# Pooled-query attention with a routed expert: score and value matmuls on four 64x64 tiles, chunk by chunk in turn

## The chip, the cores and the metric

One core of a Trainium2 chip runs the whole program, everything in float32. The metric is the time of one execution on the device in microseconds (us), lower is better. Five engines work side by side, each through its own instructions in order: TensorE (PE; its weight loads are listed apart as PEld), VectorE (DVE), ScalarE (ACT), GpSimd (POOL) and SyncE (SP), which here issues DMAs. TensorE writes into PSUM, from which ScalarE and VectorE read.

## The reference

Attention on queries that are averaged two by two, 8 batches of 8 heads, 1152 keys, head dimension 64. Then, for each batch, the 128 of 576 tokens with the highest gate score go through a two-layer expert and are added back.

```python
def _attn_ref(q, k, v):
    B, H, S, D = q.shape                     # 8, 8, 1152, 64
    scale = 1.0 / np.sqrt(D)
    q_pool = q.reshape(B, H, S // 2, 2, D).mean(axis=3)
    scores = scale * np.matmul(q_pool, k.transpose(0, 1, 3, 2))
    scores = scores - np.max(scores, axis=-1, keepdims=True)
    attn = np.exp(scores)
    attn = attn / (np.sum(attn, axis=-1, keepdims=True) + 1e-09)
    return np.matmul(attn, v).astype(np.float32)
...
def _moe_ref(x, w_gate, w1, w2, capacity):   # x: 8, 576, 512; w1: 512 x 1024; capacity 128
    scores = np.einsum('bsd,d->bs', x, w_gate)
    out = x.copy()
    for b in range(B):
        top_idx = np.argpartition(-scores[b], capacity)[:capacity]
        xe = x[b, top_idx]
        h = np.maximum(xe @ w1, 0.0)
        ye = h @ w2
        g = 1.0 / (1.0 + np.exp(-scores[b, top_idx]))
        out[b, top_idx] = x[b, top_idx] + g[:, None] * ye
```

## The kernel before

Two heads of a batch form a pair; there are 32 pairs. A pair lies in the 128 partitions as 2 heads of 64: kT and qT hold the transposed keys and pooled queries, head j in the rows 64j to 64j+63. The 576 queries of a pair are worked through in two halves of 288 (`s` is 0 or 1), so there are 64 halves, numbered h in `run`. The 1152 keys are 9 chunks of 128.

`scores` takes a half through all 9 chunks. For each chunk and head, a matmul with 64 rows of kT as weights (64 rows by 128 columns of the array) gives the transposed scores of 128 keys by 288 queries; the two heads use the two halves of the array's rows and write into the two banks of one PSUM tile. ScalarE turns the tile into exponentials (L763) in `p`. There is no maximum subtracted; at the end a count of sums outside bounds decides whether a second, general version (`_any_scores`) has to run, which it doesn't with these inputs. `weighted` takes a half through the 9 chunks again: with the values as weights (128 rows by 64 columns) and `p` as the moving operand, the two heads use the two halves of the array's columns and accumulate in one PSUM bank, which ScalarE copies out (L779). A float32 matmul is two instructions on TensorE, each with its weight load, so each of the two runs has 36 matmuls in the profile.

PSUM has one pool, `psum`, with 4 tiles of two banks each, that is all 8 banks; `banks()` (L893) hands them out in turn, to scores, values, the sums' matmul, the transposes and the expert alike. A tile is used again when its last reader is done.

The order is written out by hand in `run`; each engine works through its part of it in order. One turn h of the loop issues:

- `scores(h)`; `gated(h-3)`, a small reduction on VectorE of gate products, and for the second half of a pair another (L880); after a batch's last pair it starts that batch's routing;
- `folded(h)`: GpSimd adds p's first and second group of three chunks (L788, three sums), VectorE folds the third group and then those sums over the keys (L793, two instructions), and adds up (L802). The first of these folds reads the chunks 6 to 8, the second the three sums of GpSimd;
- `multiplied(h-2)`: GpSimd multiplies attention outputs by the gate weights (L825);
- where h is even, `prepare_pair` for the next pair: keys transposed on VectorE (L727), queries summed on GpSimd (L733) and transposed on VectorE (L739);
- `weighted(h-1)` and `drained(h-1)`: VectorE transposes the copied values into `avb` (L815);
- where h-1 was a pair's second half, `normalized`: a matmul merges the sums (L836), ScalarE copies them out (L846, two instructions), VectorE takes reciprocals (L853), GpSimd scales (L855, the tile `x`), and SyncE stores `x` in the next turn;
- `units`: each batch in routing does its next piece, the newest batch first.

The routing of a batch is a generator, `routed`, in pieces: the gate scores are brought into a row (L916, L920 and DMAs through memory), VectorE compares them to find ranks (L970, L979, L989), over three turns, and in the third makes five `pick` matrices from the ranks (L1012); a turn later TensorE multiplies these by token numbers (L1022) and ScalarE reads out indices (L1030, L1032); GpSimd gathers the tokens with an indirect DMA (L1034); later come four transposes (L1048) and their copy (L1051), the first expert layer (L1059, 64 matmuls, ReLU L1067), and the second (L1072, 16 matmuls, read by L1092), a scaled sum and a scatter. The last batch's routing, and what is left of the one before, run after the loop, the pieces of both interleaved by hand; there the gate scores become a row through matmuls (L943, L950, L671).

Of the kernel before, what the change touches and what calls it, by code (L numbers as in the profile page):

```python
# [10 lines left out]
P = 128  # L11
BLK = 32

G = 3
F32 = mybir.dt.float32
I32 = mybir.dt.int32
AF = mybir.ActivationFunctionType
ALU = mybir.AluOpType
# [516 lines left out]
class _Plain:  # L535
# [10 lines left out]
    def __init__(self, ctx, tc, q, k, v, moe_w_gate, moe_w1, moe_w2, capacity, out):  # L546
        self.tc, self.nc = tc, tc.nc
        self.q, self.k, self.v, self.out = q, k, v, out
        self.w_gate_in, self.w1_in, self.w2_in = moe_w_gate, moe_w1, moe_w2
        B, H, S, D = q.shape  # L550
        self.B, self.H, self.S, self.D = B, H, S, D
        self.Sp = S // 2
        self.Dm = H * D
        self.F = moe_w1.shape[1]
        self.NC = S // P
        self.NPAIR = H // 2
        self.HALF = self.Sp // 2
        self.QB = self.Sp // BLK
        self.HB = self.HALF // BLK
        self.KB = S // BLK  # L560
        self.NF = self.Sp // P
        self.TAIL = self.Sp - self.NF * P
        self.NT = self.NF + 1
        self.ND = self.Dm // P
        self.NFC = self.F // P
        self.NG = self.NC // G
        self.scale = 0.5 / math.sqrt(D)
        self.slots = [(s, min(P, capacity - s)) for s in range(0, capacity, P)]

        assert tuple(out.shape) == (B, self.Sp, self.Dm)  # L570
        assert 2 * D == P and D == 2 * BLK and H == 2 * self.NPAIR
        assert S == self.NC * P and self.NC == self.NG * G and self.NG == 3
        assert self.HALF == self.HB * BLK and self.HALF <= 512
        assert 0 < self.TAIL < P and self.Dm == self.ND * P and self.Dm <= 512
        assert self.F == self.NFC * P and self.NFC % 4 == 0
        assert all(w > 1 for _, w in self.slots) and capacity < self.Sp

        def pool(name, bufs, **kw):
            return ctx.enter_context(tc.tile_pool(name=name, bufs=bufs, **kw))

        self.const = pool("const", 1)
        self.load = pool("load", 2)
        self.work = pool("work", 2)
        self.small = pool("small", 4)
        self.ffn = pool("ffn", 2)
        self.dram = pool("dram", 2, space=bass.MemoryType.DRAM)
        psum = bass.MemoryType.PSUM
        self.psum = pool("psum", 4, space=psum)
        self.constants()

    def quarters(self):
# [152 lines left out]
            for a, z in parts:  # L744
                of(a, z)

    def scores(self, half):

        nc, pair, n = self.nc, half["pair"], self.HALF
        qs = slice(half["s"] * n, (half["s"] + 1) * n)  # L750
        p = half["p"] = self.work.tile([P, self.NG, G, 2, n], F32, name="p")
        for c in range(self.NC):
            sc = self.banks()
            for j in range(2):
                rows = slice(j * self.D, (j + 1) * self.D)
                nc.tensor.matmul(  # L756
                    sc[:, j, 0:n],
                    lhsT=pair["kT"][rows, c * P : (c + 1) * P],
                    rhs=pair["qT"][rows, qs],
                    start=True,  # L760
                    stop=True,
                )
            nc.scalar.activation(p[:, c // G, c % G, :, :], sc[:, :, 0:n], AF.Exp, scale=self.scale)  # L763

    def weighted(self, half):

        nc, n = self.nc, self.HALF
        av = self.banks()[:, 0, :]
        for c in range(self.NC):
            for j in range(2):  # L770
                nc.tensor.matmul(  # L771
                    av[j * self.D : (j + 1) * self.D, 0:n],
                    lhsT=half["pair"]["v"][:, j, c, :],
                    rhs=half["p"][:, c // G, c % G, j, :],
                    start=(c == 0),
                    stop=(c == self.NC - 1),
                )
        half["av"] = self.small.tile([P, n], F32, name="av", bufs=2)
        nc.scalar.copy(half["av"][:, :], av[:, 0:n])  # L779

    def folded(self, half):

# [25 lines left out]

    def drained(self, half):

        pair, hb = half["pair"], self.HB
        if half["s"] == 0:
            pair["avb"] = self.work.tile([P, self.QB, BLK], F32, name="avb")
        ns = slice(half["s"] * hb, (half["s"] + 1) * hb)
        self.nc.vector.transpose(  # L815
            pair["avb"][:, ns, :].rearrange("p n d -> p (n d)"), half["av"][:, :]
        )

    def multiplied(self, half):
# [329 lines left out]
    def run(self):  # L1149
        nc = self.nc  # L1150
        pairs = [(b, hp) for b in range(self.B) for hp in range(self.NPAIR)]
        n_halves = 2 * len(pairs)
        halves = []
        self.routing = []
        first = ((4, self.KB // 2, self.KB), (self.HB, self.QB))
        upcoming = self.load_pair(*pairs[0], parts=first, other=nc.scalar)
# [2 lines left out]
        loaded = self.load_pair(*pairs[1]) if len(pairs) > 1 else None  # L1159
        weights = self.weight_loads()  # L1160
        for h in range(n_halves + 1):
            if h < n_halves:
                n, s = divmod(h, 2)
                if s == 0:
                    pair = upcoming
                    if pair["hp"] == 0:
                        xs = self.dram.tile([self.Sp, self.Dm], F32, name="xs")
                        part = self.ffn.tile([P, self.NPAIR, self.QB], F32, name="part")
                    pair.update(xs=xs, part=part)
                else:  # L1170
                    loaded = self.load_pair(*pairs[n + 2]) if n + 2 < len(pairs) else None
                    if n > 0:
                        self.stored(halves[h - 2]["pair"])
                if h > 1:
                    next(weights, None)
                half = {"pair": pair, "s": s}
                halves.append(half)
                self.scores(half)
                if h > 2:
                    self.gated(halves[h - 3])  # L1180
                self.folded(half)
                if h > 1:
                    self.multiplied(halves[h - 2])
                if s == 0 and loaded:
                    upcoming = loaded
                    self.prepare_pair(upcoming)
            else:
                if h > 2:
                    self.gated(halves[h - 3])
                self.multiplied(halves[h - 2])  # L1190
                self.units()
            if h > 0:
                done = halves[h - 1]
                self.weighted(done)
                self.drained(done)
            if h == n_halves:
                self.multiplied(done)
                self.gated(halves[h - 2])
            if h > 0 and done["s"] == 1:
                self.normalized(done["pair"])  # L1200
            if h < n_halves:
                self.units()
        for _ in weights:
# [92 lines left out]
```

## Time and profile before

| | |
|---|---|
| median of 3 runs | 747.36 us (747.1 to 750.39) |
| the profiled execution | 747.73 us |
| its span in the profile | 746.0 us |
| granted TensorE clock, mean | 0.999 |
| TensorE matmuls, busy | 728.5 us, 5465 instructions |
| VectorE, busy | 518.8 us, 760 instructions |
| GpSimd, busy | 429.4 us, 396 instructions |
| ScalarE, busy | 388.0 us, 769 instructions |
| score matmuls L756 | 2304, busy 299.7 us |
| value matmuls L771 | 2304, busy 293.5 us |
| exponentials L763, 128x576 | 576, mean 685 ns |
| copies of values L779, 128x288 | 64, mean 400 ns |
| folds L793 | 128, means 1969 and 1951 ns |
| sums on GpSimd L788, 128x576 | 192, mean 1413 ns |

The span runs from the first to the last instruction of the program in the profile; the time on the device holds 1.7 us more. Matmuls are pipelined, and the length of one reaches from its start to the end of its passage through the array, so a run of n matmuls is read by the starts. A row of the timeline merges neighbours of the same line: start, length from the first start to the last end, engine, line, operation, tiles, shapes and count; in brackets the idle time of the engine before, and who ended it. In a row of windows the columns are the stretch, its length, and busy time and count of an engine, followed by clock, DMA share and GB/s.

### The profile page before, as it was taken

To read this page: it belongs to the slowest core of one execution; us is meant where nothing else is said; L and a number is where in the kernel's file an instruction comes from. 1 tells how busy PE (TensorE), PEld (TensorE's weight loads), DVE (VectorE), ACT (ScalarE), POOL (GpSimd) and SP (SyncE) were. 2 spreads that over 40 slices of the span, in tenths; PEclk is the share of its full clock that TensorE was granted. 3 is DMA by queue.
4 is the path that set the end of the run, shared out by engine and by line. 5 is a ranking of instruction groups with operands and counts; after the bars stand their busy time and mean duration, and the time that the engine had idled before them with its cause. 6 is when DMAs were issued, how large, how long until landed. Compare 5 with 4: busy or idle time off the path is not lost. (4 is left out here: it accounts for less than half of the span.)

```text
span 746.0 us, 14111 instructions
## 1 busy us (share of the span) xinstructions
PE 728.5 (98%) x5465; PEld 490.6 (66%) x5465; DVE 518.8 (70%) x760; ACT 388.0 (52%) x769; POOL 429.4 (58%) x396
## 2 busy tenths in 40 slices
PE   6899999999999999999999999999999999999986
PEld 4566666677566675676756767566676677666764
DVE  1766668977389753997549975498855978469640
ACT  3566666654465644666336664465535664366320
POOL 5666666664566736657556466465655655376520
PEclk9999999999999999999999999999999999999999
DMA  8999998995298646978279682995929966271130
GB/s 129 152 193 186 178 188 121 155 140 126 49 163 138 98 108 83 159 108 127 80 113 151 86 126 81 144 146 85 109 84 152 145 99 110 68 115 17 31 95 33
DMA packets 459310, 87.09 MB, mean 117 GB/s; under 512 B 455520, under 2 KB 455520, under 8 KB 458976
## 3 DMA queue, kind: packets, MB, share of 16 engines
q1 hardware_dynamic: 455008, 81.53, 70.4%
q0 software_dynamic: 1280, 4.20, 2.1%
q8 instruction: 45, 0.74, 0.5%
q10 hardware_dynamic: 2944, 0.36, 0.3%
q14 instruction: 33, 0.27, 0.1%
HBM read 74.50 MB, written 20.99 MB: 128 GB/s over the span
## 5 line engine op out<-in xcount | busy, mean ns | idle before, releaser
L763 ACT ACTIVATE p<-ps 128x576 f32<-128x576 f32 x576 | 319.9, 685 | 19.6 <-PE ps L756 12.8
L788 POOL TENSOR_TENSOR acc<-p 128x576 f32<-128x576 f32 x192 | 265.8, 1413 | 90.2 <-ACT p L763 89.7
L756 PE MATMUL ps<-qT,kT 64*128 64x288 f32 x2304 | 299.7, 410 | 7.7 <-DVE qT L739 7.7
L771 PE MATMUL ps<-p,v_sb 128*64 128x288 f32 x2304 | 293.5, 409 | 0.0
L756 PEld LDWEIGHTS ps<-qT,kT 64*128 64x128 f32 x2304 | 223.7, 188 | 73.1 <-issue 18.5
L771 PEld LDWEIGHTS ps<-p,v_sb 128*64 128x64 f32 x2304 | 159.8, 137 | 125.6 <-ACT p L763 24.2
L793 DVE TRANSPOSE_TENSOR_REDUCE fold<-p 128x54 f32<-128x1728 f32 x64 | 126.0, 1969 | 122.8 <-ACT p L763 122.8
L793 DVE TRANSPOSE_TENSOR_REDUCE fold<-acc 128x54 f32<-128x1728 f32 x64 | 124.9, 1951 | 55.6 <-POOL acc L788 55.6
L779 ACT COPY av<-ps 128x288 f32<-128x288 f32 x64 | 25.6, 400 | 214.9 <-PE ps L771 214.9
L855 POOL TENSOR_TENSOR x<-avb,rec 128x576 f32<-128x576 f32 x32 | 37.0, 1158 | 146.0 <-DVE rec L853 133.9
L1059 PEld LDWEIGHTS ps<-xeT,w 128*128 128x128 f32 x512 | 58.0, 192 | 3.7 <-issue 2.6
L1059 PE MATMUL ps<-xeT,w 128*128 128x128 f32 x512 | 59.7, 277 | 0.7 <-ACT xeT L1051 0.7
L1072 PE MATMUL ps<-w,hT 128*128 128x512 f32 x128 | 57.0, 597 | 0.0
L825 POOL TENSOR_TENSOR prod<-avb,w_gate 128x288 f32<-128x288 f32 x64 | 50.9, 795 | 3.9 <-DVE avb L815 3.9
L733 POOL TENSOR_TENSOR qp<-qb 128x576 f32<-128x576 f32 (+1 forms) x33 | 45.0, 1362 | 9.8 <-DMA qb<-in_q_dram 9.7
L727 DVE STREAM_TRANSPOSE kT<-kb 128x1152 f32<-128x1152 f32 (+3 forms) x34 | 44.0, 1296 | 4.6 <-DMA kb<-in_k_dram 4.3
L1012 DVE TENSOR_SCALAR pick<-slot_f,rank 128x128 f32<-128x128 f32 (+1 forms) x40 | 41.9, 1110 | 0.4
L1072 PEld LDWEIGHTS ps<-w,hT 128*128 128x128 f32 x128 | 23.6, 190 | 26.3 <-issue 26.1
L1067 ACT ACTIVATE hT<-ps 128x512 f32<-128x512 f32 x16 | 9.6, 597 | 50.6 <-PE ps L1059 50.6
L880 DVE TENSOR_TENSOR part<-red,rec 128x18 f32<-128x18 f32 x32 | 33.6, 1050 | 1.1
L739 DVE STREAM_TRANSPOSE qT<-qp 128x576 f32<-128x576 f32 (+1 forms) x33 | 23.8, 721 | 10.9 <-POOL qp L733 10.9
L815 DVE STREAM_TRANSPOSE avb<-av 128x288 f32<-128x288 f32 x64 | 29.0, 453 | 1.1 <-ACT av L779 1.1
(71 smaller groups left out, 276.4 us busy)
## 6 DMA issues: line engine op xcount, KB each, us to landing
v_sb<-in_v_dram SPq DMA_DIRECT2D x64, 288.0 KB, 5.0
kb<-in_k_dram SPq DMA_DIRECT2D x124, 144.0 KB, 4.3
qb<-in_q_dram SPq DMA_DIRECT2D x124, 144.0 KB, 4.6
xs<-x SPq DMA_DIRECT2D x128, 72.0 KB, 3.1
out_dram<-xs SPq DMA_DIRECT2D x8, 1152.0 KB, 5.6
w<-in_moe_w_dram SPq DMA_DIRECT2D x8, 512.0 KB, 5.0
sc_row<-row SPq DMA_DIRECT2D x7, 288.0 KB, 3.3
qb<-in_q_dram ACTq DMA_DIRECT2D x4, 72.0 KB, 2.7
```

The source lines that it names most:

```text
L727: nc.vector.transpose(pair["kT"][:, a * BLK : z * BLK], pair["k"][:, a:z, :].rearrange("p n d -> p (n d)"),)
L733: nc.gpsimd.tensor_tensor(out=qp[:, a:z, :], in0=pair["q"][:, a:z, 0, :], in1=pair["q"][:, a:z, 1, :], op=ALU.add,)
L756: nc.tensor.matmul(sc[:, j, 0:n], lhsT=pair["kT"][rows, c * P : (c + 1) * P], rhs=pair["qT"][rows, qs], start=True, stop=True,)
L763: nc.scalar.activation(p[:, c // G, c % G, :, :], sc[:, :, 0:n], AF.Exp, scale=self.scale)
L771: nc.tensor.matmul(av[j * self.D : (j + 1) * self.D, 0:n], lhsT=half["pair"]["v"][:, j, c, :], rhs=half["p"][:, c // G, c % G, j, :], star ...
L788: nc.gpsimd.tensor_tensor(out=acc[:, u, :], in0=units[:, 0, u, :], in1=units[:, 1, u, :], op=ALU.add)
L793: nc.vector.tensor_reduce(fold[:, a, :], of.rearrange("p u (m d) -> p (u m) d", d=BLK), AX.X, ALU.add, apply_transpose=True,)
L825: self.nc.gpsimd.tensor_tensor(out=pair["prod"][:, ns, :], in0=pair["avb"][:, ns, :], in1=self.w_gate[:, hp : hp + 1, :].broadcast_to([P, ...
L855: nc.gpsimd.tensor_tensor(out=x[:, :, :], in0=pair["avb"][:, :, :], in1=rec[:, :].unsqueeze(2).broadcast_to([P, self.QB, BLK]), op=ALU.mult,)
L1012: nc.vector.tensor_scalar(out=pick[0:rows, t, 0:w], in0=self.slot_f[0:rows, s0 : s0 + w], scalar1=rank[0:rows, t : t + 1], scalar2=None, o ...
L1059: nc.tensor.matmul(pv[:, f, 0:w], lhsT=self.w1[:, c, (f0 + f) * P : (f0 + f + 1) * P], rhs=xeT[:, c, 0:w], start=(c == 0), stop=(c == self ...
L1072: nc.tensor.matmul(ps[0:w, 0 : self.Dm], lhsT=hT[:, f, 0:w], rhs=self.w2[:, f, :], start=(f == 0), stop=(f == self.NFC - 1),)
```

## The change

`scores` and `weighted` become one function, `attended(half, done)`. For each chunk it issues the scores of the present half, the exponential, and then the values of the half before, for the same chunk. Each matmul is split in two: the scores by keys (64 of the chunk's 128, that is 64 columns of weights), the values by keys too (64 rows of weights), so that every matmul has a 64x64 tile of weights and the same 288 columns to move. A chunk's scores are then four matmuls on the four quarters of the array, and so are its values. The two halves of the keys of the values accumulate in two PSUM banks; both are copied out in one instruction, 576 columns instead of 288, and GpSimd adds them (a new instruction in `drained`), ahead of the transpose. PSUM is divided into two pools: 2 tiles of two banks for scores and everything else, and 2 for values. In `run` the values of h-1 now come ahead of `gated`, `folded`, `multiplied` and `prepare_pair`. In the turn after the last half, `units` comes ahead of the values.

```diff
@@ -585,7 +585,8 @@
-        self.psum = pool("psum", 4, space=psum)
+        self.psum = pool("psum", 2, space=psum)
+        self.ps_av = pool("ps_av", 2, space=psum)
@@ -744,39 +745,45 @@
-    def scores(self, half):
...
-    def weighted(self, half):
...
+    def attended(self, half, done):
+        nc, n = self.nc, self.HALF
+        quarters = [(slice(e * self.D, (e + 1) * self.D), e, j) for e in range(2) for j in range(2)]
+        if half:
+            pair = half["pair"]
+            qs = slice(half["s"] * n, (half["s"] + 1) * n)
+            p = half["p"] = self.work.tile([P, self.NG, G, 2, n], F32, name="p")
+        if done:
+            av = self.ps_av.tile([P, 2, 512], F32, name="av")
         for c in range(self.NC):
+            if half:
+                sc = self.banks()
+                for keys, e, j in quarters:
+                    rows = slice(j * self.D, (j + 1) * self.D)
+                    nc.tensor.matmul(
+                        sc[keys, j, 0:n],
+                        lhsT=pair["kT"][rows, c * P + keys.start : c * P + keys.stop],
+                        rhs=pair["qT"][rows, qs],
+                        start=True,
+                        stop=True,
+                    )
+                nc.scalar.activation(
+                    p[:, c // G, c % G, :, :], sc[:, :, 0:n], AF.Exp, scale=self.scale
+                )
+            if done:
+                for keys, e, j in quarters:
+                    nc.tensor.matmul(
+                        av[j * self.D : (j + 1) * self.D, e, 0:n],
+                        lhsT=done["pair"]["v"][keys, j, c, :],
+                        rhs=done["p"][keys, c // G, c % G, j, :],
+                        start=(c == 0),
+                        stop=(c == self.NC - 1),
+                    )
+        if done:
+            done["av"] = self.small.tile([P, 2, n], F32, name="av", bufs=2)
+            nc.scalar.copy(done["av"][:, :, :], av[:, :, 0:n])
@@ -808,12 +815,16 @@
     def drained(self, half):
-        pair, hb = half["pair"], self.HB
+        pair, hb, av = half["pair"], self.HB, half["av"]
+        total = self.small.tile([P, self.HALF], F32, name="av_sum", bufs=2)
+        self.nc.gpsimd.tensor_tensor(
+            out=total[:, :], in0=av[:, 0, :], in1=av[:, 1, :], op=ALU.add
+        )
...
-            pair["avb"][:, ns, :].rearrange("p n d -> p (n d)"), half["av"][:, :]
+            pair["avb"][:, ns, :].rearrange("p n d -> p (n d)"), total[:, :]
@@ -1175,29 +1187,27 @@
-                self.scores(half)
-                if h > 2:
-                    self.gated(halves[h - 3])
+            if h == n_halves:
+                self.units()
+            done = halves[h - 1] if h else None
+
+            self.attended(half, done)
+            if h > 2:
+                self.gated(halves[h - 3])
+            if half:
                 self.folded(half)
-                if h > 1:
-                    self.multiplied(halves[h - 2])
-                if s == 0 and loaded:
-                    upcoming = loaded
-                    self.prepare_pair(upcoming)
...
+            if h > 1:
                 self.multiplied(halves[h - 2])
-                self.units()
-            if h > 0:
-                done = halves[h - 1]
-                self.weighted(done)
+            if half and half["s"] == 0 and loaded:
+                upcoming = loaded
+                self.prepare_pair(upcoming)
+            if done:
                 self.drained(done)
-            if h == n_halves:
-                self.multiplied(done)
-                self.gated(halves[h - 2])
-            if h > 0 and done["s"] == 1:
-                self.normalized(done["pair"])
+                if h == n_halves:
+                    self.multiplied(done)
+                    self.gated(halves[h - 2])
+                if done["s"] == 1:
+                    self.normalized(done["pair"])
             if h < n_halves:
                 self.units()
```

## The prediction

> **What bounds the kernel now.** I read the page first, for the shares of the engines; then the timeline of one stretch in the middle of the run; then the list of waits; then the timelines of VectorE and GpSimd over the same stretch, because a reordering of TensorE's work changes when theirs can begin.
>
> ```profile
> span 746.0 us, 14111 instructions
> ...
> PE 728.5 (98%) x5465; PEld 490.6 (66%) x5465; DVE 518.8 (70%) x760; ACT 388.0 (52%) x769; POOL 429.4 (58%) x396
> ```
>
> TensorE has work for 98% of the span, so whatever changes its busy stretch changes the time. The timeline shows what this stretch is made of:
>
> ```profile
> 301.19 4.64 PE L756 MATMUL ps<-qT,kT 64*128 64x288 f32 x36
> ...
> 305.76 4.59 PE L771 MATMUL ps<-p,v_sb 128*64 128x288 f32 x36
> ...
> 310.27 0.41 PE L836 MATMUL ps<-sum,merge 128*128 128x36 f32 x2
> 310.39 0.40 ACT L779 COPY av<-ps 128x288 f32<-128x288 f32 x1 [3.35 <-PE ps L771]
> 310.62 4.64 PE L756 MATMUL ps<-qT,kT 64*128 64x288 f32 x36
> 310.72 0.56 ACT L846 ACTIVATE sums<-ps,tiny 64x18 f32<-64x18 f32 x2
> ...
> 315.18 4.59 PE L771 MATMUL ps<-p,v_sb 128*64 128x288 f32 x36
> ...
> 319.70 4.64 PE L756 MATMUL ps<-qT,kT 64*128 64x288 f32 x36
> ```
>
> Columns are start, length, engine, line, operation, count. A half is 36 score matmuls and 36 value matmuls; each half starts 9.08 us after the one before where nothing stands between (310.62 to 319.70) and 9.43 us where the sums' matmul L836 does (301.19 to 310.62). The pace inside a run comes from a piece cut out of one:
>
> ```profile
> 321.74 2.59 PE L756 MATMUL ps<-qT,kT 64*128 64x288 f32 x20
> ...
> 329.02 1.23 PE L1022 MATMUL ps<-meta,pick 128*128 128x3 f32 x9
> ```
>
> One such matmul has a length of 0.40, so 20 of them take (2.59 - 0.40)/9 = 0.243 us per pair: two run at once, in the two halves of the array. The expert matmuls L1072, one at a time with 512 columns, follow each other by 0.43 us, and 288/512 of that is 0.242. So the pair is paced by the array, not by loading or issuing. 36 pairs at 0.243 are 8.74 us; the other 0.34 us of a direct half are the changes between the two forms of matmul. From 28.3 to 694.3 us, 62 halves, TensorE has no other pause. VectorE looks idle by its 70%, but not in the stretch in which a batch's tokens are ranked:
>
> ```profile
> 297.99 1.98 DVE L793 TRANSPOSE_TENSOR_REDUCE fold<-p 128x54 f32<-128x1728 f32 x1 [9.62 <-ACT p L763]
> ...
> 323.31 6.01 DVE L1012 TENSOR_SCALAR pick<-slot_f,rank 128x128 f32<-128x128 f32 x5
> 329.24 0.43 DVE L878 TENSOR_REDUCE red<-prod 128x9 f32<-128x288 f32 x1
> ```
>
> ```profile
> 297.90:329.30 31.40, 30.70 (x55) 1.00 1.06 143
> ```
>
> In the second view (VectorE's own windows) it is busy 30.70 of 31.40 us, beginning with the fold of the half whose scores started at 292.11. The picks end at 329.3, and the last of the matmuls that read them (L1022, from 329.02) begins at about 330.0. There are some 0.6 us to spare.
>
> **The change, part by part.** *Matmuls.* Each of 72 matmuls of a half becomes two on a 64x64 tile with the same 288 columns. If four run at once, a quad takes the pair's 0.243 us, and a half keeps its 36 steps, 8.74 us. I take this, since both neighbours are in the trace: two tiles that share rows (the values) and two that share columns (the scores) both go at full pace. What goes is the change of form: 0.34 us per direct half. Where L836 or an expert stage stands between, some 0.15 of it stays as the way back into the attention form (9.43 - 9.08 = 0.35 is paid for L836 as now), so 0.19 is saved. Of 62 halves, 31 have L836 behind them and 6 an expert stage: 25 x 0.34 + 37 x 0.19 = **-15.5 us**.
>
> [...]
>
> *Twice the instructions.* Eight loads and matmuls have to issue in 0.243 us, 30 ns each. The trace shows only that 61 ns each is kept up (4 per pair), and over the 128 instructions of an expert stage 56 ns. Bounds: nothing, and a doubling of every step (8.74 x 62 = +542 us). I take nothing, because the pace above is exactly the array's, so the issuing was not at its limit; the other end is a rival.
>
> *Two PSUM buffers instead of four* for scores and everything else. L836 then writes into the buffer of chunk 7, and what comes two tiles later needs its reader L846 to be done. Now L846 ends 311.28, which is 1.34 us after the start of the last value pair (305.76 + 4.59 - 0.41 = 309.94). The copy before it grows from 288 columns to 576 (0.40 to about 0.69, the length of an exponential of 576), and an exponential is still ahead of it (0.1): 1.73 us. Where only L836 stands between, its successor needs the buffer a chunk later (0.97 us) and waits under 0.1. With the four transposes L1048 behind, the next scores would start at 1.3: 0.17 for the last exponential's buffer and 0.4 for L846. With L916 and L1072 behind, L1072 would start at 0.97: 0.17 and 0.72. Per batch 0.07 + 0.57 + 0.89 = 1.5 us, 7 batches: **+10.6 us**, bounds 0 (should the exponentials' early part take it up) and 14.
>
> *Chunks in turn.* The last exponential of a half now comes at the half's end. In the stretch above, the first fold started 5.88 us after its scores' first matmul (297.99 - 292.11); with 9 chunks of 0.97 us (scores and values of a chunk, two quads each) it starts at 8.74 + 0.44 = 9.18. VectorE works through the same list in order, without a pause to catch up in, so its end, the picks, comes 3.3 us later. TensorE arrives at L1022 some 0.9 us earlier (two direct halves, one with L836, one up to L1022, less 0.1 for the buffers). Minus the 0.6 to spare: L1022 waits 3.6 us, and in TensorE's queue the next half's scores and all else stand behind it. 7 such stretches lie inside the loop: **+25 us**. Bounds: a pick takes 1.2 us here while GpSimd runs sums beside it, but in the tail, with GpSimd quiet, five took 1.06 together:
>
> ```profile
> 718.12 1.06 DVE L1012 TENSOR_SCALAR pick<-slot_f,rank 128x128 f32<-128x128 f32 x5
> ```
>
> Five quick picks would take 4.9 us off and end the wait: 0. Above: the added sums on GpSimd hold up each pick and fold once more (0.8 us twice), and after a pause of 6 us at the start the first six pairs took 0.48 instead of 0.24, 1.4 us if it happens after this one: 7 x 6.6 = 46. I take the middle one because GpSimd will be just as full there: three sums of 1.4, a product of 0.8, a query sum of 1.4, now another 0.8.
>
> *The added sum* (L825's form, 128x288, 0.8 us x 64) lies on GpSimd, busy 58%, behind the value copy; in the loop only x and the products come later for it, which have a half to spare. In the tail it is on the path. There the chain is: last copy, transpose, product, ranks, picks:
>
> ```profile
> 705.25 0.48 DVE L815 STREAM_TRANSPOSE avb<-av 128x288 f32<-128x288 f32 x1 [1.13 <-ACT av L779]
> ```
>
> It starts 0.29 (longer copy) + 0.8 + 0.1 later, and with two buffers the count's matmul L1127 waits for the read of the old expert result, 0.5: **+1.7 us**. The first 28 us end with the second pair's queries, which come from memory: 0. DMAs and their queues issue the same transfers in the same order.
>
> Sum, against the profiled execution's own 747.7 us (746.0 span and 1.7 around it; the median of the three is 747.36): 747.7 - 15.5 + 10.6 + 25 + 1.7 = **769.5 us**.
>
> **Rivals.** *The late folds cost nothing* (other side). If picks miss GpSimd's sums, L1022 waits under 0.46 us a batch; that is the point at which -15.5 + 10.6 + 1.7 = -3.2 is used up. Then 744.5, and 734 if the buffers wait for nothing: 740. For it: a pick's price hangs on where GpSimd is just then. Against it: GpSimd's list there grows.
>
> *Four tiles don't run at once, or can't be fed.* Two at a time: 747.7 + 542 = 1290; a quad of 0.30 instead of 0.243: +127, 875. For it: no row shows more than two tiles, or instructions faster than 56 ns for long. Against it: the exact pace of the array in both present forms.
>
> *The alternation itself costs.* If the present 0.34 us belongs to the change of operands and not of tile form, a half pays it nine times instead of once: 8 x 0.34 x 62 = +169, 917. For it: no row has scores and values in one form. Against it: L836, followed by L1022 with other operands in the same form, keeps the 0.11 us of its neighbours.
>
> **How the numbers follow.** Full pace with late folds 0.57, between 752 and 790 for itself. Late folds free 0.22. Not four at once 0.08, alternation 0.06. The remaining 0.07 is a draw of gain and waits near the old time. What a measurement can tell from no change is 0.5%, 743.6 to 751.1. Faster: 0.21. Within: 0.10. Slower: 0.69. The range reaches from the middle of the rival on the other side, 738, to 795; below it lies some 0.06, above it 0.14.
>
> **What would show it.** Right: runs of 72 matmuls in which four start within some 10 ns, quads every 0.243 us, no pause between scores and values; VectorE's first fold 9.2 us behind its half's start; TensorE waiting some 3.6 us for picks at L1022, seven times; short waits for L846 and L920's buffers. Wrong: quads above 0.25 us, a pause at every chunk, L1022 without a wait, or waits of the scores for the exponentials inside a half, which I count at nothing because a chunk (0.97 us) exceeds an exponential (0.69) and its buffer is wanted again only 1.94 us later.

## The result, and the profile after

The changed kernel is slower: a median of 782.44 us over 4 runs (781.3 to 783.15) against 747.23 us (746.41 to 750.39), a ratio of 1.0462 [1.0428, 1.0495]. The profiled execution took 783.15 us. This is the top of its page; the rows of the second part are tenths of 40 slices, here the clock that TensorE was granted:

```profile
span 781.4 us, 23357 instructions
...
PE 742.7 (95%) x10073; PEld 465.9 (60%) x10073; DVE 494.8 (63%) x760; ACT 448.0 (57%) x769; POOL 478.6 (61%) x460
...
PEclk8999999899998999989999899998999989999998
```

The clock has become part of the story: a dip about every 95 us, which is once per batch. The granted clock averages 0.965 instead of 0.999. TensorE's share fell to 95%, so there are pauses as well. First the attention itself, in the timeline of TensorE (start, length, engine, line, operation, tiles, shapes, count; in brackets the idle time before and who ended it):

```profile
310.42 0.67 PE L765 MATMUL ps<-qT,kT 64*64 64x288 f32 x8
310.90 0.66 PE L777 MATMUL av<-p,v_sb 64*64 64x288 f32 x8
311.39 0.66 PE L765 MATMUL ps<-qT,kT 64*64 64x288 f32 x8
```

Each row holds eight instructions, two for each of four tiles, and the rows follow each other by 0.485 us, so a quad (four instructions, one for each tile) starts every 0.2425 us. The single starts show the four of a quad within some 20 ns, and 72 quads (two halves' worth, scores and values of nine chunks) in 17.29 us from first to last start, where 71 x 0.2425 is 17.22. So four tiles do run at once, eight loads and matmuls do issue in the 0.2425 us of a quad, and going from scores to values costs nothing. A direct half takes 8.78 us (the starts of its first scores are 301.64 and 310.42) where it took 9.08, and one with L847 behind it 9.19 (310.42 to 319.61) where it took 9.43. The same timeline where a batch's tokens are picked:

```profile
336.65 0.67 PE L777 MATMUL av<-p,v_sb 64*64 64x288 f32 x8
337.24 0.41 PE L847 MATMUL ps<-sum,merge 128*128 128x36 f32 x2
338.05 0.35 PE L1033 MATMUL ps<-meta,pick 128*128 128x3 f32 x2 [0.39 <-DVE pick L1023]
338.71 0.38 PE L1033 MATMUL ps<-meta,pick 128*128 128x3 f32 x2 [0.31 <-DVE pick L1023]
340.06 0.39 PE L1033 MATMUL ps<-meta,pick 128*128 128x3 f32 x2 [0.97 <-DVE pick L1023]
340.81 1.11 PE L1033 MATMUL ps<-meta,pick 128*128 128x3 f32 x4 [0.36 <-DVE pick L1023]
341.84 1.24 PE L765 MATMUL ps<-qT,kT 64*64 64x288 f32 x8
342.86 1.18 PE L777 MATMUL av<-p,v_sb 64*64 64x288 f32 x8
...
347.41 0.66 PE L765 MATMUL ps<-qT,kT 64*64 64x288 f32 x8
```

Two things are to be seen. L1033 (the old L1022) waits for one pick after another, and the next half's scores stand behind it: from L847 to the scores pass 4.6 us. And the scores and values behind them then follow each other by 1.02 and 0.96 us where 0.485 was the pace: for 44 matmuls, 5.3 us, TensorE runs at half its clock, until about 347.1. The windows of all engines say the same (stretch, its length, then busy time and count of PE, PEld, DVE, ACT and POOL, clock, DMA share, GB/s), and the third row, of TensorE alone, bounds the stretch:

```profile
329.00:338.00 9.00, 8.65 (x142) 5.20 (x134) 8.51 (x17) 6.74 (x13) 8.92 (x10) 1.00 0.86 135
338.00:347.00 9.00, 7.32 (x54) 4.67 (x58) 8.93 (x11) 2.05 (x8) 2.66 (x3) 0.63 0.57 99
```

```profile
340.31:347.14 6.83, 6.47 (x50) 0.50 0.43 81
```

The clock already falls while the last picks are read. The trace has six such stretches of 6.83 us inside the loop, behind the first six batches' picks, and one of 3.41 behind the seventh's.

VectorE and GpSimd are both full ahead of the picks. Their rows, from the fold with which the batch's last ranking begins:

```profile
310.86 1.98 DVE L800 TRANSPOSE_TENSOR_REDUCE fold<-p 128x54 f32<-128x1728 f32 x1 [10.44 <-ACT p L772]
...
335.41 1.12 DVE L1000 SCALAR_TENSOR_TENSOR tie<-sc_row,gate_sc,before 64x64 f32<-64x64 f32 x1
336.78 4.16 DVE L1023 TENSOR_SCALAR pick<-slot_f,rank 128x128 f32<-128x128 f32 x5
340.87 0.43 DVE L889 TENSOR_REDUCE red<-prod 128x9 f32<-128x288 f32 x1
```

```profile
333.68 4.14 POOL L795 TENSOR_TENSOR acc<-p 128x576 f32<-128x576 f32 x3
337.78 0.79 POOL L836 TENSOR_TENSOR prod<-avb,w_gate 128x288 f32<-128x288 f32 x1
338.54 1.38 POOL L734 TENSOR_TENSOR qp<-qb 128x576 f32<-128x576 f32 x1
339.89 0.78 POOL L820 TENSOR_TENSOR av_sum<-av 128x288 f32<-128x288 f32 x1
```

The fold starts 9.22 us after its half's first score (301.64). The picks end at 340.9, just after GpSimd's last row here. They are shorter than before, 4.16 us for the five instead of 6.01 (L1012 at 323.31 in the view before), and the single rows of the two engines say why. Four of the picks end at 337.90, 338.65, 340.01 and 340.75, each 0.08 to 0.09 us behind the end of one of GpSimd's last four instructions here, and the fifth, with GpSimd done, takes 0.27 us. Before, all five picks ended so behind an instruction of GpSimd: the three sums, the product and the query sum. So a later start lets the picks miss two of the sums, and the added sum gives them one instruction more to wait behind.

Where the 35.4 us between the spans (781.4 - 746.0) lie, each from the starts in the two traces, the first as what is left (the shorter halves above are its direct evidence):

| place | us | how read |
|---|---|---|
| steady attention, changes of form gone | -14.5 | remainder |
| waits for the two PSUM buffers | +10.7 | after L927, 0.977 to the next start (before 0.111 or 0.194), 7 times; after L1059, 0.725 (0.203), 6 times; from L847 to L927 or L1059, 0.22 (0.11), 13 times |
| waits for the picks | +20.6 | from the last L847 to the next scores 4.44 to 4.63, in the seventh batch 2.93 (before 1.32); of this, the ten starts of L1033 span 3.51 and 2.09 (1.10) |
| half clock after the picks | +17.2 | the two-half block after each takes 19.77 to 19.93 instead of 17.30; the last one 1.69 more |
| tail, from the last L847 | +1.86 | 43.16 (41.30) |
| start | -0.5 | the third half begins at 27.8 (28.3) |

### The profile page after: what moved, and what is told of

The parts are those of the page before. It is cut to its first block, busy times and chain, and to the rows that moved or that the text cites. A ratio compares the mean times of both kernels' runs of the same rounds, so it can differ in the third digit from the quotient of the medians.

```text
span 781.4 us, 23357 instructions
## 1 busy us (share of the span) xinstructions
PE 742.7 (95%) x10073; PEld 465.9 (60%) x10073; DVE 494.8 (63%) x760; ACT 448.0 (57%) x769; POOL 478.6 (61%) x460
## 5 line engine op out<-in xcount | busy, mean ns | idle before, releaser
L772 ACT ACTIVATE p<-ps 128x576 f32<-128x576 f32 x576 | 374.5, 651 | 184.3 <-PE ps L765 173.6
L765 PE MATMUL ps<-qT,kT 64*64 64x288 f32 x4608 | 396.1, 417 | 9.6 <-DVE qT L740 5.7
L777 PE MATMUL av<-p,v_sb 64*64 64x288 f32 x4608 | 389.0, 410 | 0.0
L765 PEld LDWEIGHTS ps<-qT,kT 64*64 64x64 f32 x4608 | 172.5, 136 | 125.2 <-issue 12.4
L777 PEld LDWEIGHTS av<-p,v_sb 64*64 64x64 f32 x4608 | 178.1, 136 | 110.6 <-issue 9.4
L836 POOL TENSOR_TENSOR prod<-avb,w_gate 128x288 f32<-128x288 f32 x64 | 51.3, 801 | 3.3 <-DVE avb L826 3.3
L820 POOL TENSOR_TENSOR av_sum<-av 128x288 f32<-128x288 f32 x64 | 51.1, 798 | 3.2 <-ACT av L786 3.2
L786 ACT COPY av<-av 128x576 f32<-128x576 f32 x64 | 40.5, 633 | 4.0 <-PE av L777 4.0
L1000 DVE SCALAR_TENSOR_TENSOR tie<-sc_row,gate_sc,before 128x128 f32<-128x128 f32 (+1 forms) x40 | 33.4, 835 | 0.0
L1103 ACT ACTIVATE y<-ps,own_gate 128x512 f32<-128x512 f32 x7 | 4.8, 688 | 45.7 <-PE ps L1083 45.7
L826 DVE STREAM_TRANSPOSE avb<-av_sum 128x288 f32<-128x288 f32 x64 | 29.1, 454 | 1.1 <-POOL av_sum L820 1.1
```

The source lines that it names most:

```text
L765: nc.tensor.matmul(sc[keys, j, 0:n], lhsT=pair["kT"][rows, c * P + keys.start : c * P + keys.stop], rhs=pair["qT"][rows, qs], start=True, ...
L777: nc.tensor.matmul(av[j * self.D : (j + 1) * self.D, e, 0:n], lhsT=done["pair"]["v"][keys, j, c, :], rhs=done["p"][keys, c // G, c % G, j, :],
L786: nc.scalar.copy(done["av"][:, :, :], av[:, :, 0:n])
L820: self.nc.gpsimd.tensor_tensor(out=total[:, :], in0=av[:, 0, :], in1=av[:, 1, :], op=ALU.add)
L836: self.nc.gpsimd.tensor_tensor(out=pair["prod"][:, ns, :], in0=pair["avb"][:, ns, :], in1=self.w_gate[:, hp : hp + 1, :].broadcast_to([P, ...
```

## The experiments

The theory: the four tiles bring what the form changes cost, and late picks take it back twice, as a wait and as a lowered clock. The rivals: the alternation or the small buffers are to blame, or GpSimd's added sum.

**The matmuls read the picks a turn later.** In the changed kernel:

```diff
+            if b < self.B - 1:
+                yield True
             ps = self.banks()[:, 0, 0:3]
```

> The changed kernel, but TensorE's product of the picks (and all later pieces of a batch's routing) comes one turn later, except for the last batch; nothing else is moved. Theory (late folds make the picks late, TensorE waits for them and then runs at half clock): both go, 20.5 us of waits and 17.2 us of half clock, so 782.4 - 37.7 = 745, between 742 and 749; granted clock back from 0.965 to 0.99 or more. Rival (the half clock belongs to four tiles at once, not to the pause): only the waits go, about 762, clock stays near 0.97. Rival (VectorE is overloaded by the change as such and the wait moves to another place): no better than 775.

Measured: 764.6 us, 1.0241 [1.022, 1.0263], clock 0.996. The wait for the picks and the dips of the clock behind it are gone, and 18 us with them, but not 37: the forecast of 745 is missed. A batch's queue on VectorE stayed as late, and TensorE now met it elsewhere. Its list of waits (who waited for whom: us in total, times, longest) has these:

```profile
PE ps L765 <- DVE qT L740: 17.6, 7, 5.8
...
PEld ps L927 <- ACT sums L857: 7.3, 6, 1.2
```

The scores now wait 1.9 to 2.1 us a batch, in six of them, for the next pair's transposed queries (the 5.8 us are the start of the program). The tail is 4.0 us longer than the changed kernel's. VectorE's and GpSimd's timelines show why VectorE is late:

```profile
350.07 5.99 DVE L891 TENSOR_TENSOR part<-red,rec 128x18 f32<-128x18 f32 x1
```

```profile
349.77 4.13 POOL L795 TENSOR_TENSOR acc<-p 128x576 f32<-128x576 f32 x3
353.87 0.79 POOL L836 TENSOR_TENSOR prod<-avb,w_gate 128x288 f32<-128x288 f32 x1
354.62 1.40 POOL L734 TENSOR_TENSOR qp<-qb 128x576 f32<-128x576 f32 x1
355.99 0.79 POOL L820 TENSOR_TENSOR av_sum<-av 128x288 f32<-128x288 f32 x1
```

An operation on 18 columns, which takes 0.18 us in 13 of its 32 places in this run, lasts 5.99 us and ends with GpSimd's fifth instruction in a row. It does so, within 0.2 us, once in each of six batches; in the kernel before it lasted up to 3.86 us, in the changed kernel at most 1.26.

**TensorE kept at work while it waits.** Three matmuls of 512 columns into an unused bank of the picks' PSUM tile:

```diff
-            ps = self.banks()[:, 0, 0:3]
+            fill = self.banks()
+            if b < self.B - 1:
+                for c in range(3):
+                    nc.tensor.matmul(fill[:, 1, :], lhsT=self.ident[:, :],
+                                     rhs=self.w1[:, c, 0:512], start=True, stop=True)
+            ps = fill[:, 0, 0:3]
```

> The changed kernel with work added: ahead of the product of the picks TensorE gets three matmuls of 512 columns into an unused PSUM bank, in each of the seven batches inside the loop (6 instructions of 0.43 us, 2.6 us per batch, 18 us in all). Theory (TensorE is only waiting there, and the pause lowers the clock): the added work fits into the wait and keeps the clock up, so the time falls by up to 17.2 us, to 765 to 769. Rival (the clock drop has nothing to do with the pause): 782, or more where the added work doesn't fit, up to 800.

Measured: 764.92 us, 1.0257 [1.0219, 1.0294], clock 0.994. The timeline of TensorE, same place:

```profile
331.30 0.41 PE L847 MATMUL ps<-sum,merge 128*128 128x36 f32 x2
331.66 2.84 PE L1034 MATMUL ps<-w,ident 128*128 128x512 f32 x6
334.34 1.26 PE L1043 MATMUL ps<-meta,pick 128*128 128x3 f32 x10
335.53 0.71 PE L765 MATMUL ps<-qT,kT 64*64 64x288 f32 x8
336.06 0.67 PE L777 MATMUL av<-p,v_sb 64*64 64x288 f32 x8
336.55 0.66 PE L765 MATMUL ps<-qT,kT 64*64 64x288 f32 x8
```

TensorE still gets on only when the picks are done, but the scores and values behind them follow by 0.49 us at once (0.53 the first time). Some 18 us of work for nothing were added, and the kernel is 17.5 us faster (782.44 - 764.92). This separates the two parts of the loss: the clock's is the 17.2 us read from the trace.

**The four tiles without the alternation.** The kernel before, its order and its one pool of four PSUM tiles, with the matmuls on 64x64 tiles and GpSimd's sum:

```diff
-            for j in range(2):
+            for keys, e, j in self.quads():
...
-                    sc[:, j, 0:n],
-                    lhsT=pair["kT"][rows, c * P : (c + 1) * P],
+                    sc[keys, j, 0:n],
+                    lhsT=pair["kT"][rows, c * P + keys.start : c * P + keys.stop],
...
-                    av[j * self.D : (j + 1) * self.D, 0:n],
-                    lhsT=half["pair"]["v"][:, j, c, :],
-                    rhs=half["p"][:, c // G, c % G, j, :],
+                    av[j * self.D : (j + 1) * self.D, e, 0:n],
+                    lhsT=half["pair"]["v"][keys, j, c, :],
+                    rhs=half["p"][keys, c // G, c % G, j, :],
```

> Four 64x64 tiles and the added sum on GpSimd, but in the order of the kernel before (all scores of a half, then all values of the half before) and with its one PSUM pool of four tiles. Theory (four tiles run at full pace and save the changes of form; the loss comes from the order and the buffers): 747.2 - 15 + 1.3 in the tail = 733.5, plus up to 4 us where TensorE now comes 1 us too early for the picks: 733 to 738, faster than before. Rival (the gain came only from the turn by turn order, or twice the instructions cost something of themselves): 745 or more.

Measured: 739.61 us (739.13 to 743.16), 0.991 [0.9881, 0.994], faster than the kernel before. Its TensorE rows, a value run directly behind a score run, and a half later:

```profile
302.13 4.54 PE L774 MATMUL ps<-p,v_sb 64*64 64x288 f32 x72
306.61 0.41 PE L843 MATMUL ps<-sum,merge 128*128 128x36 f32 x2
306.95 4.60 PE L759 MATMUL ps<-qT,kT 64*64 64x288 f32 x72
311.36 0.92 PE L774 MATMUL ps<-p,v_sb 64*64 64x288 f32 x12
```

Scores to values takes 4.41 us (306.95 to 311.36), 18 steps of 0.2425 and no more than 0.05 on top. A batch takes 88.5 us instead of 90.1. It misses its forecast by 1.6 us: the first batch's picks still came 1.9 us late, and the tail is 2.2 us longer (43.46 for 41.30). So the change of tiles is worth having, and runs, not turns, keep the folds early (a direct half's first fold starts 5.86 us after its first score, 5.88 before).

**The alternation without the four tiles.** The changed kernel's order and pools, with the old forms of matmul and no added sum:

```diff
-                for keys, e, j in quarters:
+                for j in range(2):
...
-                        sc[keys, j, 0:n],
-                        lhsT=pair["kT"][rows, c * P + keys.start : c * P + keys.stop],
+                        sc[:, j, 0:n],
+                        lhsT=pair["kT"][rows, c * P : (c + 1) * P],
```

> The changed kernel's order and PSUM pools, but each matmul in the form of before (64 rows by 128 columns for scores, 128 by 64 for values), without the added sum. Theory (the change of tile form costs 0.17 us each time, here 18 times in a half): 0.34 x 9 x 62 = 190 us more than the changed kernel's matmuls, less the waits for picks, which go because a half lasts 3 us longer: 782 + 190 - 38 = 934, between 900 and 960. Rival (what costs is only the first matmul after a wait, not the change of form): 745 to 785.

Measured, one run: 932.17 us, clock 0.999. The timeline:

```profile
399.64 0.71 PE L777 MATMUL av<-p,v_sb 128*64 128x288 f32 x4
400.27 0.76 PE L765 MATMUL ps<-qT,kT 64*128 64x288 f32 x4
400.96 0.71 PE L777 MATMUL av<-p,v_sb 128*64 128x288 f32 x4
```

A chunk takes 1.32 us instead of 0.97: the two changes of form cost the same 0.35 us as before, but nine times a half. What the present 0.34 us paid for was the form of the tile, not the operands: the price is there with two forms (932 us) and gone with one (in the changed kernel 72 quads of scores and values in turn took 17.29 us from first to last start, and 71 x 0.2425 is 17.22).

**Routing ahead of the folds.** In the changed kernel, `units()` moved ahead of `folded`, so that VectorE does its part of the picks first:

```diff
+            if h < n_halves:
+                self.units()
             if half:
                 self.folded(half)
...
-            if h < n_halves:
-                self.units()
```

> The changed kernel, but a turn issues its piece of the routing ahead of the folds instead of at the turn's end, so VectorE does the comparisons and picks while it would otherwise wait for the half's last exponential. Theory (the picks are late because they stand behind folds that now start 3.3 us later): the wait for picks and the half clock go, 782.4 - 37.7 = 745; as the run with the routing one turn later showed that a wait can come back at the keys and queries (2.0 us a batch) or at the sums, up to 760. Clock 0.99 or more. Rival (VectorE and GpSimd have too much to do in this stretch in any order): 762 or more, as there.

Measured: 816.8 us, 1.0925 [1.0896, 1.0953], clock 0.958: a miss. The list of waits names what had been overlooked:

```profile
POOL xe L1106 <- ACT y L1103: 125.8, 7, 20.9
DVE fold L800 <- POOL acc L795: 106.8, 28, 12.8
```

A piece of the routing also holds GpSimd's sum of the expert's output, which waits for TensorE. Ahead of `folded`, it stands in front of the sums for the folds, 18 us a batch. A moved piece carries every queue it issues to; this run says nothing on the theory.

**Three buffers for scores, one for values.**

```diff
-        self.psum = pool("psum", 2, space=psum)
-        self.ps_av = pool("ps_av", 2, space=psum)
+        self.psum = pool("psum", 3, space=psum)
+        self.ps_av = pool("ps_av", 1, space=psum)
```

> The changed kernel with PSUM divided the other way: three tiles for scores and everything else, one for the values. Theory (waits behind the sums' reader cost 11 us with two tiles): the waits after the row's and the transposes' matmuls go (9 us), but the values of each half that follows directly have to wait for the copy of the last, 0.5 us x 25 = 12 us; and a later TensorE waits less for picks, 1.0 us x 7: 782.4 - 9 + 12 - 7 = 778, between 771 and 787. Rival (buffers play no part): the waits after those matmuls stay as they are.

Measured: 772.44 us, 1.0328 [1.0303, 1.0352], clock 0.977. The next matmul after L927 and L1059 starts 0.11 and 0.20 us later again, so those waits were the buffers' indeed. Most of it comes back, since the values now wait for the copy of the last half's; the list of waits, and TensorE's timeline behind a direct half:

```profile
PEld av L777 <- ACT av L786: 24.3, 36, 0.8
```

```profile
310.52 0.71 PE L777 MATMUL av<-p,v_sb 64*64 64x288 f32 x8 [0.33 <-ACT av L786]
```

The 24.3 us are waits of the weight loads, and part of them is covered; the half that begins here takes 9.74 us instead of 9.19. Taken half by half, the gain of 10.1 us between the two spans lies elsewhere: 2.8 us in the halves that end with the picks and 7.3 us in those behind them, where the clock falls in five batches instead of seven; all other halves of the loop together gain 1.5 us, which the start and the tail lose again (0.7 and 0.5).

**No added sum.** The values of only the first half of the keys go on; those of the second half stay out of the result.

```diff
-        total = self.small.tile([P, self.HALF], F32, name="av_sum", bufs=2)
-        self.nc.gpsimd.tensor_tensor(out=total[:, :], in0=av[:, 0, :], in1=av[:, 1, :], op=ALU.add)
...
-            ..., total[:, :]
+            ..., av[:, 0, :]
```

> The changed kernel without the added sum on GpSimd: of the two halves of the keys only the first one's values are transposed and go on, the second's are left out of the result. Theory (the sum matters little: one more hold-up of 0.8 us in the stretch of the picks, and 0.9 us in the tail): 782.4 - 7 x 0.8 - 0.9 = 776, between 771 and 781. Rival (GpSimd's added work is what makes the picks late): 765 or less.

Measured: 765.0 us, 1.0221 [1.0204, 1.0238], clock 0.983. That is the rival's number, and the theory's 771 to 781 is missed: the sum bears 17.4 us. VectorE's rows show how:

```profile
330.16 0.39 DVE L996 SCALAR_TENSOR_TENSOR tie<-sc_row,gate_sc,before 64x64 f32<-64x64 f32 x1
...
330.80 3.62 DVE L1019 TENSOR_SCALAR pick<-slot_f,rank 128x128 f32<-128x128 f32 x5
```

The row ahead of the picks takes 0.39 instead of 1.12 us, the picks 3.62 instead of 4.16, and TensorE waits 1.4 us a batch on average instead of 2.9 (from the last sums' matmul to the next scores, less the 1.32 of before). After the shorter wait the clock is still lowered in 5 batches, but in three of them for only 24 to 28 matmuls instead of 44: some 1.7 us lost (7 quads x 0.24) instead of 2.5. In all, 10.6 of the 17.4 us are waits for picks and 1.5 the tail; the rest is nearly all the clock.

**The late folds alone.** The kernel before, `weighted` and `drained` issued ahead of `folded`. TensorE's order stays as it was; VectorE's list alone changes:

```diff
+                if h > 0:
+                    done = halves[h - 1]
+                    self.weighted(done)
+                    self.drained(done)
                 self.folded(half)
...
-            if h > 0:
+            if h == n_halves:
```

> The kernel before, in which only VectorE's order is changed: the transpose of the values (which waits for the end of the half's value matmuls and their copy) stands ahead of the folds instead of behind them. TensorE's, ScalarE's and GpSimd's own orders, tile forms and buffers are as before, no sum is added, and the folds start about as late as in the changed kernel. Theory (late folds alone make the picks late): TensorE waits 1.5 to 3 us a batch for the picks and loses 1.5 to 2.5 us a batch at half clock: 747.5 + 7 x 3 to 7 x 5.5 = 768 to 786. Rival (late folds do nothing without the added sum on GpSimd, as the run without the sum, which gained 17 us, could be read): 747 to 750.

Measured: 761.43 us (760.18 to 765.25), 1.0203 [1.0179, 1.0227], clock 0.991. TensorE's timeline where the picks are read:

```profile
333.11 0.41 PE L836 MATMUL ps<-sum,merge 128*128 128x36 f32 x2
333.35 0.36 PE L1022 MATMUL ps<-meta,pick 128*128 128x3 f32 x2
333.96 0.38 PE L1022 MATMUL ps<-meta,pick 128*128 128x3 f32 x2 [0.24 <-DVE pick L1012]
335.31 0.81 PE L1022 MATMUL ps<-meta,pick 128*128 128x3 f32 x5 [0.97 <-DVE pick L1012]
```

The rival is out: without new tiles, buffers or sum, a later place in VectorE's list costs 14 us (761.43 against 747.2). But it is less than the theory asked for, though a direct half's first fold now starts 10.09 us after its first score, later even than in the changed kernel. From L836 to the next scores it is 0.95 to 1.53 us longer in six batches and no longer in the seventh, 7.0 us in all (1.0 a batch), and the clock drops after only 3 of the 6 pauses, which costs about 5 us. Why the wait is so short stands in VectorE's list:

```profile
332.03 3.61 DVE L1012 TENSOR_SCALAR pick<-slot_f,rank 128x128 f32<-128x128 f32 x5
```

Three picks end behind GpSimd's last sum, its product and its query sum, and two are free, at 0.27 us: the five take 3.61 us instead of 6.01, and that takes back over half of the delay.

**One instruction for the five picks**, in the changed kernel:

```diff
-            for t, rows in tiles:
-                nc.vector.tensor_scalar(
-                    out=pick[0:rows, t, 0:w], in0=self.slot_f[0:rows, s0 : s0 + w],
-                    scalar1=rank[0:rows, t : t + 1], scalar2=None, op0=ALU.is_equal)
+            nc.vector.tensor_tensor(
+                out=pick[:, :, 0:w],
+                in0=self.slot_f[:, s0 : s0 + w].unsqueeze(1).broadcast_to([P, NT, w]),
+                in1=rank[:, :].unsqueeze(2).broadcast_to([P, NT, w]),
+                op=ALU.is_equal)
```

> The changed kernel, but the five picks are made by one instruction on VectorE (a comparison of two broadcast tiles, 640 columns) instead of five. Theory (each pick is held up by a sum that runs on GpSimd; five hold-ups make up most of the 4.2 us): one hold-up and some 0.7 us of work, done 2 to 3 us earlier, so the wait shrinks from 3.0 to under 1 us a batch and the clock loss with it: 782.4 - 7 x 2.3 - 7 x 2 = 752, between 746 and 758. Rival (the picks are simply work that starts late): 5 x 0.21 us of work is no more than one of 0.7, so little changes: 775 or more.

Measured: 766.36 us (762.93 to 768.72), 1.0257 [1.0229, 1.0285], clock 0.98; between the two numbers. VectorE's row:

```profile
329.40 1.72 DVE L1022 TENSOR_TENSOR pick<-slot_f,rank 128x640 f32<-128x640 f32 x1
```

The five picks take 1.72 us instead of 4.16, TensorE waits 1.2 us a batch instead of 2.9, and the clock still drops in 5 of 7 batches, for 24 to 28 matmuls (up to 1.7 us) each: a pause does not have to be long to be followed by one.

**Two tries at better runs.** In the kernel with four tiles and without the alternation, ScalarE waited 28.4 us in all to copy values out, since GpSimd's sum held the two buffers of `av`. So `av` got four buffers, and then the one pick as well:

```diff
-        half["av"] = self.small.tile([P, 2, n], F32, name="av", bufs=2)
+        half["av"] = self.small.tile([P, 2, n], F32, name="av", bufs=4)
```

> The run with four tiles in the old order, but four instead of two buffers for the copied values. There the copy of a batch's values waited for GpSimd's sum, and exponentials and scores behind it. Theory: that wait (up to 3.1 us on ScalarE, 0.2 to 0.3 us on TensorE, two or three times a batch) goes: 739.6 - 2 = 737.5, between 736 and 739. If ScalarE's wait was covered: 739.6.

> Four 64x64 tiles in the order of the kernel before with four buffers for copied values (the run that took 744 us, with a wait for picks in the first batch of 2.9 us and a lowered clock there), and the one instruction for the five picks. Theory: no wait for picks is left, clock 0.998 throughout: 735 to 737, and steady; faster than the kernel before by 1.4%. If something else lowers the clock there: 740 to 745.

Measured: 744.45 us (737.22 to 747.12, 12 runs), 0.9954 [0.9934, 0.9973], and 743.19 us (739.48 to 746.23), 0.9949 [0.9927, 0.9971]. The first misses its forecast; the second lies where it was put in case something else lowers the clock. Neither is better than the 739.61 of plain runs. In the profiled run of the first (742.12) ScalarE's wait is gone, but the first batch's picks come later still: 6.66 us from the sums' matmul to the next scores, 3.32 in plain runs, and a lowered clock behind it. In the trace of the second no picks are waited for, and inside the loop only one stretch of half clock is left, 3.4 us from 29.2 us on. The mean clock of its runs varies from 0.989 to 0.996, with no order between clock and time; why both medians lie above that of the plain runs stays open, and since the intervals of the first and of the plain runs touch, so does whether the difference is real. The lowest median found is that of the four tiles in plain runs, 0.9% below the kernel before.

## Why the prediction was right, and where it was mis-sized

- **Four at once, fed, no cost of turns.** Held: 0.2425 us a quad, no pause between scores and values. -14.5 is left for it in the table, -15.5 was predicted.
- **Two buffers.** +10.7 for +10.6; after L927 and L1059 it was 0.87 us and 0.52 us late, predicted 0.89 and 0.57. Three buffers for the scores took these waits away.
- **Late folds, late picks.** The fold came 9.22 us after its half's start, 9.2 predicted. The place and the mechanism held: TensorE stood before the matmuls of the picks seven times. The term of +25 should have been +37.8. This is the step that was mis-sized, and three errors in it, of both signs, partly cancel. That the time fell inside the range owes something to this: had late folds alone cost the 25 us, the 10.6 us of waits that go with the added sum and the 17.2 of the clock would have come on top, some 798 in all, above the range.
  - "L1022 waits 3.6 us" for late folds alone was too much: they cost 1.0 us a batch where only the fold was moved in the old kernel, and 1.4 where the sum was taken out of the new one. "VectorE works through the same list in order, without a pause to catch up in, so its end, the picks, comes 3.3 us later" has the fault: the list got shorter, since the picks, which start later, miss two of GpSimd's sums and took 3.6 us in both runs instead of 6.01. The rival on the other side was right in that much.
  - The wait measured in the changed kernel, 2.9 us a batch and 20.6 in all, is near 3.6 only because the added sum, put at nothing in the loop, makes up the other half of it (1.5 us).
  - "After a pause ... 1.4 us if it happens after this one" stood in the upper bound alone, and "I take the middle one" left it out. It happened after every pause, and cost 2.47 to 2.63 us in six of them and 1.69 in the last: 17.2 us. The 1.4 us came from a pause with six slow pairs; here 44 matmuls, eleven quads, were slow.
- **The added sum.** "In the loop only x and the products come later for it" was wrong: VectorE's rows beside it came later too, and the picks with them. Taking it out brought 17.4 us, mostly through these rows and the clock behind the longer wait. The 17.4 are not a further term: all but the tail's 1.5 lie within the 37.8. The tail's +1.7 was right (+1.86).
- **The rivals.** Late folds do cost (1.0203 alone). The alternation costs only with two forms of tile (932 us). The size of the whole, 783.15 for 769.5, is the 12.8 us of the third term (37.8 - 25); the other terms together are off by 0.8.

## What to carry to other kernels

When the bound engine gets its work in another order, follow the engine that runs nearly without slack through its whole list: a reader moved from the middle of a run to its end is late by that much, and what stands behind it by more or less, according to what it now runs beside (here the picks got shorter by 1.9 to 2.4 us). Price a wait of the bound engine with what follows it, the clock included; filling the wait with useless matmuls brought as much here (17.5 us) as shortening it (16.1 with one pick, 17.4 without the sum). And try the parts of a change apart: here the tiles gained and the order lost.

## What the runs showed of the hardware

- In the changed kernel's first six batches a pause in which TensorE ran ten tiny matmuls over 3.5 us (single idle times up to 0.97) was followed by 5.1 to 5.4 us of matmuls at half pace, 0.48 us a quad. Half that waiting (1.4 us a batch, without the added sum) was followed by slow matmuls in 5 batches, 24 to 28 of them in three of these. With 2.6 us of dense matmuls in the pause, the quads behind it followed each other by 0.2425 us and the run's mean clock was 0.994. The granted clock in the traces before and after is 1.0 or 0.5, with nothing between.
- In these two traces the granted clock changes at times that are whole multiples of 3.413 us apart; after the change the lowered stretches behind the picks begin 95.57 us, 28 such steps, apart, and last two of them in six batches (6.83 us) and one in the seventh (3.41 us). The loss did not shrink in proportion to the pause: waits of about 1.2 us with one pick still cost 24 to 28 slow matmuls, up to 1.7 us, in 5 of 7 batches.
- VectorE operations were stretched while GpSimd worked: 18 columns from 0.18 to 5.99 us, and a pick from 0.27 to as long as the GpSimd instruction beside it lasted (0.8 or 1.4 us), ending 0.08 to 0.09 us behind it. L891, the operation on 18 columns, ended in the run with the later matmuls not with one GpSimd instruction but with the fifth in a row (356.06 us, the fifth 356.02).
- The loads of 64x64 tiles, two of which share rows, stayed hidden behind running matmuls at 30 ns an instruction (eight in 0.2425 us), which the trace before had not shown.
